# Sparse attention scores on one NeuronCore: four key blocks as two products of 64 keys or as one of 128

## The chip, the cores and the metric

The kernel runs on one core of one Trainium2 chip. The metric is the device time of one execution in microseconds (us), of which the median over several runs counts. A profile is one further execution, recorded by the hardware profiler.

## The reference

The reference is a block-sparse attention followed by a mixture of experts. There are 4 batches, 8 heads, 768 positions and 64 values per head, all in 32-bit floats. Positions form 24 blocks of 32. A query block attends to its neighbours, to the first and the last block, and to three drawn blocks; the first and the last query block attend to everything.

```python
scores = scale * np.matmul(q, k.transpose(0, 1, 3, 2))
mask = np.abs(blk_i - blk_j) <= window
mask = mask | (blk_i == 0) | (blk_j == 0) | (blk_i == n_blocks - 1) | (blk_j == n_blocks - 1)
for qb in range(n_blocks):
    for kb in sampled_blocks[qb]:
        mask[qb * block:(qb + 1) * block, kb * block:(kb + 1) * block] = True
scores = np.where(mask, scores, -1000000000.0)
...
attn = np.exp(scores)
attn = attn / (np.sum(attn, axis=-1, keepdims=True) + 1e-09)
return np.matmul(attn, v)
```

The result, as 3072 rows of 512 values, goes through a gate that picks one of 8 experts for each row. The expert is two matrix products (512 to 1024 and back) with a rectifier between them, and its result is scaled by the gate's weight.

## The kernel before

Attention comes first and the experts second; the same room in SBUF serves both. For one batch the 24 query blocks form six groups, numbered g. Groups 0 to 4 are full tiles of 128 queries: two query tiles (ti = 0 and 1) of two blocks each, with 64 queries to a tile. Group 5, called GL, holds the last two ordinary blocks and the two that attend to everything. GL is worked first in each batch.

The work of a group is cut into two half-steps of two head pairs each, so a batch has 12 half-steps and the kernel 48. The loop at L1271 runs over them. A head pair lies on the 128 partitions of keys and queries, one head on partitions 0 to 63 and the other on 64 to 127.

For each head pair of a full tile, plan (L288) lists the score products. The keys of a query tile are 384: 128 common to the group (xk: the first and the last block and the group's middle), 64 of its own neighbourhood (kT), and 192 drawn ones (kr: six blocks of 32, three for each query block). Keys are the stationary operand and queries the moving one, and the scores land in PSUM with the keys on the partitions. A product with 64 keys is put on the lower or the upper half of the PSUM partitions; plan calls the list of these few, and the list of products with 128 keys many. scores (L314) issues few for both head pairs at L321 and then many for both at L326, each product once for each head. Then ScalarE takes the exponential of the whole tile of scores (L331), and VectorE multiplies it by a mask (L337).

The drawn keys are brought to kr by place_keys (L515) two half-steps ahead: ScalarE copies the first three blocks of a query tile and VectorE the other three (both L528). The drawn values come from DRAM by indirect DMAs of the POOL queue (fetch_values, L488), each held back by a small copy (not_before, L500) until a given piece of work is done.

On TensorE the order is written out by hand and is the program's order. In a half-step it is: the scores of this half-step, the transposes of the next batch's keys or queries (turn, L156), the products of the previous half-step's probabilities with the values (attend, L355), and among these, in every second half-step, the transposes of a finished tile (turn_out, L437) and the gate's logits (L455). VectorE divides by the sums afterwards (divide, L415 to L421). In the last batch VectorE also works out where each row goes (early, L1239, and the functions it calls, among them count at L744).

After attention the experts run on tiles of 128 rows (layer1 at L1094, layer2 at L1108), with weights fetched two tiles ahead.

The functions that the change touches, and those that call them:

Of the kernel before, what the change touches and what calls it, by code (L numbers as in the profile page):

```python
# [17 lines left out]
def kernel(  # L18
# [12 lines left out]
    P = 128  # L31
    B, H, S, D = q.shape
# [246 lines left out]
    def parity(b, g):  # L279
        return (b * NG + order.index(g)) % 2  # L280
# [4 lines left out]
    def at_cols(tile_, a, n):  # L285
        return lambda r: tile_[r, a : a + n]

    def plan(b, g, pr):  # L288

        kT, qT = sets[b][0][:, pr, :], sets[b][1][:, pr, :]  # L290
        mine = [kr[:, parity(b, g), ti, pr, :] for ti in range(2)]
        q0 = BLK + P * g
        few, many = [], [(at_cols(xk[:, parity(b, g), pr, :], 0, P), at_cols(qT, q0, P), 0, P)]
        for ti in range(2):
            qs = at_cols(qT, q0 + D * ti, D)
            few += [(0, at_cols(kT, P * (g + ti), D), qs, P + D * ti, D), (1, at_cols(mine[ti], 0, D), qs, P + D * ti, D)]
            many.append((at_cols(mine[ti], D, P), qs, 2 * P + D * ti, D))
        return few, many

    def plan_all(b, pr):  # L300
# [970 lines left out]
    for i, (b, g, half) in enumerate(steps):  # L1271
# [17 lines left out]
        if g == GL:  # L1289
            plans = [plan_all(b, pr) for pr in prs if b > 0] + [plan_two(b, prs)]  # L1290
            *e_alls, e = scores(*plans)
            masked_two(e)
            mine = [(b, g, pr, e_alls[pr % 2] if b > 0 else None, e) for pr in prs]
        else:
            found = scores(*[plan(b, g, pr) for pr in prs])
            for e in found:
                masked(e, g)
            mine = [(b, g, pr, None, e) for pr, e in zip(prs, found)]
# [236 lines left out]
```

## Time and profile before

| what | us |
|---|---|
| timed runs: median of three | 679.02 |
| timed runs: lowest and highest | 676.74, 680.68 |
| profiled execution | 650.76 |
| its span, first to last instruction | 649.0 |
| attention in it, from the first scores of a half-step to the first expert product | 34.4 to 286.0 |
| TensorE matmul busy time | 611.7 |
| TensorE weight-load busy time | 512.0 |
| VectorE, ScalarE, GpSimd busy time | 300.9, 218.1, 184.1 |
| mean granted TensorE clock, as a share of full speed | 0.973 |

In the profile PE stands for TensorE's matmuls, PEld for its weight loads, which run beside matmuls, DVE for VectorE, ACT for ScalarE, POOL for GpSimd and SP for SyncE. A row of the groups gives the line, the engine, the operation, what it writes and reads, the shapes (partitions x elements), the count, the busy time with the mean duration of one in nanoseconds, and the idle time of the engine just before these instructions with what ended it. "issue" is a wait in which nothing that the profile shows was late. A row of the timeline gives the start, the time covered, the engine, the line, the operation, and how many neighbouring instructions of one kind it merges. A row of the waits gives the total, how often it came, and the longest.

### The profile page before, as it was taken

What the parts mean: (1) busy time and instruction counts of PE and PEld (TensorE: products, weight loads), DVE (VectorE), ACT (ScalarE), POOL (GpSimd) and SP (SyncE); (2) the same over time, 40 slices, a digit from 0 to 9 for tenths busy, and PEclk for the clock granted to TensorE, in tenths of its full rate; (3) what the DMA queues carried; (4) which work ended last, traced back from release to release, by engine and by line L of the source; (5) the groups of instructions that cost most, each with busy time, mean ns of one, the idle gap of its engine ahead of it and who ended that gap; (6) DMA issues with size and microseconds to landing.
All of it is one profiled execution on the core that took longest, in us unless ns stands there. A gap on an engine that the chain in (4) does not pass through costs nothing. (4 is left out here: it accounts for less than half of the span.)

```text
span 649.0 us, 21354 instructions
## 1 busy us (share of the span) xinstructions
PE 611.7 (94%) x8952; PEld 512.0 (79%) x8952; DVE 300.9 (46%) x966; ACT 218.1 (34%) x418; POOL 184.1 (28%) x289
## 2 busy tenths in 40 slices
PE   7789999998999997999999999999989999999994
PEld 6778888997999886987777777877869678867862
DVE  4247765765577488734920495202091024602200
ACT  2347755775677655431111011111111211111110
POOL 2047753552455344620111221011400212020210
PEclk9689999999999999699999999999999999999998
DMA  9889886987797338876888999869995799989950
GB/s 184 210 195 245 243 218 158 221 231 198 158 232 235 95 90 290 283 260 231 315 299 299 335 383 348 293 239 382 396 397 192 256 405 397 339 278 402 396 189 20
DMA packets 136249, 170.93 MB, mean 263 GB/s; under 512 B 83444, under 2 KB 83445, under 8 KB 136118
## 3 DMA queue, kind: packets, MB, share of 16 engines
q1 hardware_dynamic: 126080, 137.61, 65.4%
q0 software_dynamic: 10000, 31.59, 15.2%
q8 instruction: 80, 1.31, 0.9%
q14 instruction: 51, 0.42, 0.2%
q10 hardware_dynamic: 38, 0.00, 0.0%
HBM read 150.11 MB, written 19.33 MB: 261 GB/s over the span
## 5 line engine op out<-in xcount | busy, mean ns | idle before, releaser
L1094 PEld LDWEIGHTS hp<-around,room 128*128 128x128 f32 x1216 | 138.3, 192 | 7.3 <-issue 5.1
L1094 PE MATMUL hp<-around,room 128*128 128x128 f32 x1216 | 140.8, 276 | 1.4 <-ACT kr L1101 1.4
L1075 DVE STREAM_TRANSPOSE around<-xg 32x128 f32<-32x128 f32 x208 | 63.0, 303 | 125.9 <-PE hp L1094 95.9
L1108 PE MATMUL zp<-room,kr 128*128 128x512 f32 x256 | 112.7, 594 | 0.0
L488 POOL DMA_INDIRECT around<-v_rows,rows_of x88 | 92.6, 1052 | 63.5 <-DVE xk L513 25.3
L331 ACT ACTIVATE ea<-s 128x768 f32<-128x768 f32 x104 | 79.7, 809 | 91.1 <-PE s L326 70.7
L355 PE MATMUL op<-around,ea 128*64 128x65 f32 x2112 | 87.6, 228 | 5.2 <-DMA around<-v_rows,rows_of 3.9
L1108 PEld LDWEIGHTS zp<-room,kr 128*128 128x128 f32 x256 | 47.6, 191 | 54.6 <-issue 54.6
L355 PEld LDWEIGHTS op<-around,ea 128*64 128x64 f32 x2112 | 76.3, 140 | 13.3 <-DMA around<-v_rows,rows_of 4.5
L337 DVE TENSOR_TENSOR ea<-ea,mask 128x768 f32<-128x768 f32 x80 | 73.2, 954 | 14.8 <-ACT ea L331 14.8
L1101 ACT ACTIVATE kr<-hp 128x512 f32<-128x512 f32 x36 | 21.5, 597 | 117.4 <-PE hp L1094 109.9
L1123 POOL DMA_INDIRECT out_dram<-kr,sB x14 | 14.1, 1005 | 164.7 <-ACT kr L1113 106.1
L1113 ACT ACTIVATE kr<-zp,xg 128x512 f32<-128x512 f32 x16 | 11.0, 687 | 101.2 <-PE zp L1108 101.2
L1201 DVE STREAM_TRANSPOSE ea<-ea 32x128 f32<-32x128 f32 x84 | 21.7, 285 | 32.7 <-DMA ea<-x_rows,gB 32.0
L321 PE MATMUL s<-room 64*64 64x64 f32 x736 | 24.4, 237 | 5.3 <-DVE room L161 4.6
L1123 POOL DMA_INDIRECT out_dram<-kr,sA x5 | 5.1, 1020 | 79.6 <-ACT kr L1113 79.6
L326 PE MATMUL s<-other,kr 64*128 64x64 f32 x352 | 26.9, 266 | 0.7 <-issue 0.7
L321 PEld LDWEIGHTS s<-room 64*64 64x64 f32 x736 | 20.2, 147 | 7.3 <-issue 4.5
L326 PE MATMUL s<-room,kr 64*128 64x64 f32 x352 | 25.8, 261 | 0.0
L326 PEld LDWEIGHTS s<-other,kr 64*128 64x128 f32 x352 | 25.0, 195 | 0.8 <-issue 0.8
L326 PEld LDWEIGHTS s<-room,kr 64*128 64x128 f32 x352 | 23.9, 190 | 1.0 <-issue 1.0
L500 POOL COPY paced<-sums 1x1 f32<-1x1 f32 x42 | 7.5, 179 | 60.1 <-DVE sums L415 55.6
(338 smaller groups left out, 870.2 us busy)
## 6 DMA issues: line engine op xcount, KB each, us to landing
room<-in_moe_w_dram SPq DMA_DIRECT2D x46, 2048.0 KB
room<-in_moe_w_dram SPq DMA_DIRECT2D x16, 512.0 KB
room<-in_k_dram SPq DMA_DIRECT2D x32, 192.0 KB
room<-in_q_dram SPq DMA_DIRECT2D x32, 192.0 KB
x_rows<-xb SPq DMA_DIRECT2D x20, 256.0 KB
v_rows<-room SPq DMA_DIRECT2D x12, 260.0 KB
v_rows<-other SPq DMA_DIRECT2D x12, 260.0 KB
room<-in_v_dram SPq DMA_DIRECT2D x16, 192.0 KB
```

What stands on the lines that cost most here:

```text
L321: nc.tensor.matmul(s[j * D : (j + 1) * D, hh, a : a + n], lhsT=keys(r), rhs=queries(r), start=True, stop=True)
L326: nc.tensor.matmul(s[:, hh, a : a + n], lhsT=keys(r), rhs=queries(r), start=True, stop=True)
L331: nc.scalar.activation(e, s[:, :, : 6 * D], AF.Exp, scale=scale)
L337: nc.vector.tensor_tensor(e, e, m[:, None, :].to_broadcast([P, 2, 6 * D]), op=ALU.mult)
L355: nc.tensor.matmul(op[ti * D : (ti + 1) * D, pr % 2, hh, : D + 1], lhsT=e, rhs=values[:, (2 * pr + hh) * VW : (2 * pr + hh + 1) * VW], sta ...
L488: nc.gpsimd.indirect_dma_start(out=around[p0:, par, 1 + ti + 2 * ch, :], out_offset=None, in_=v_d[b][:, :], in_offset=bass.IndirectOffsetO ...
L1075: nc.vector.transpose(xT[d, :, t], xg[t, :DM].rearrange("p (c q) -> p c q", c=DB)[:, :, d])
L1094: nc.tensor.matmul(hp[:, m, :], lhsT=st[i]["w1"][:, c, fb * P : (fb + 1) * P], rhs=st[i]["xT"][:, c, :], start=(c == 0), stop=(c == DB - 1),)
L1101: nc.scalar.activation(hT[:, g * (FB // 2) : (g + 1) * (FB // 2), :], hp[:], AF.Relu)
L1108: nc.tensor.matmul(zp[:], lhsT=st[i]["hT"][:, fb, :], rhs=st[i]["w2"][:, fb, :], start=(fb == 0), stop=(fb == FB - 1),)
L1123: ins = nc.gpsimd.indirect_dma_start(out=to[:, :], out_offset=bass.IndirectOffsetOnAxis(ap=at, axis=0), in_=rows, in_offset=None, bounds_c ...
L1201: nc.vector.transpose(xT_u[d, :, j * P + tq * 32 : j * P + (tq + 1) * 32], xg_u[t, j, :DM].rearrange("p (c q) -> p c q", c=DB)[:, :, d],)
```

## The change

In plan, the 128 keys of a query tile's last four drawn blocks (columns 64 to 191 of kr) were one entry of many: one product with 128 keys and 64 queries. Now they are two entries of few with 64 keys each: columns 64 to 127 go to the lower half of the PSUM partitions and columns 128 to 191 to the upper half, at the same PSUM columns. The scores land where they landed before. They are issued at L321 with the other products of 64 keys, ahead of all products of many, of which one per head pair is left (xk). plan_two, which serves group GL, is not changed.

```diff
         for ti in range(2):
             qs = at_cols(qT, q0 + D * ti, D)
             few += [(0, at_cols(kT, P * (g + ti), D), qs, P + D * ti, D), (1, at_cols(mine[ti], 0, D), qs, P + D * ti, D)]
-            many.append((at_cols(mine[ti], D, P), qs, 2 * P + D * ti, D))
+            few += [(j, at_cols(mine[ti], D * (1 + j), D), qs, 2 * P + D * ti, D) for j in range(2)]
         return few, many
```

## The prediction

> **What bounds the kernel now.** I read the page first: shares of busy time, the groups of the changed lines, the DMA queues.
>
> ```profile
> span 649.0 us, 21354 instructions
> PE 611.7 (94%) x8952; PEld 512.0 (79%) x8952; DVE 300.9 (46%) x966; ACT 218.1 (34%) x418; POOL 184.1 (28%) x289
> ...
> q8 instruction: 80, 1.31, 0.9%
> ...
> L326 PEld LDWEIGHTS s<-room,kr 64*128 64x128 f32 x352 | 23.9, 190 | 1.0 <-issue 1.0
> ```
>
> TensorE sets the time. The chain of waits holds only the last 1.2 us and tells nothing of attention. The q8 row matters later: TensorE's own instructions arrive by DMA, 16 KB a packet. The trace shows each f32 product as two weight loads and two matmuls, so the 352 loads of a 128-key block are 176 products.
>
> Next, the timeline of TensorE's weight loads in one half-step of scores, which shows the pace of both kinds:
>
> ```profile
> 125.31 0.14 PEld L321 LDWEIGHTS s<-other,kr 64*64 64x64 f32 x2
> 125.33 0.17 PEld L321 LDWEIGHTS s<-other 64*64 64x64 f32 x2
> 125.37 0.14 PEld L321 LDWEIGHTS s<-other,kr 64*64 64x64 f32 x2
> 125.38 0.17 PEld L321 LDWEIGHTS s<-other 64*64 64x64 f32 x2
> 125.43 0.14 PEld L321 LDWEIGHTS s<-other,kr 64*64 64x64 f32 x2
> ...
> 125.55 0.14 PEld L321 LDWEIGHTS s<-other,kr 64*64 64x64 f32 x2
> 125.75 0.30 PEld L326 LDWEIGHTS s<-other,xk 64*128 64x128 f32 x4
> 125.97 0.53 PEld L326 LDWEIGHTS s<-other,kr 64*128 64x128 f32 x8
> 126.42 0.31 PEld L326 LDWEIGHTS s<-other,xk 64*128 64x128 f32 x4
> ```
>
> One load takes 0.14 us, yet four (two rows of x2) start every 0.06 us: four 64x64 quarters of the array work side by side. The single records give 58.3 ns a round of four. The eight kr loads of 128 keys take from 125.97 to 126.42, 0.446 us: 112 ns a round of two. The burst runs at the pace of its loads.
>
> Then the waits of TensorE, and one stall in its timeline:
>
> ```profile
> PE op L355 <- DMA around<-v_rows,rows_of: 3.9, 4, 1.9
> PE s L321 <- issue: 3.7, 5, 1.5
> PE xr L437 <- DVE xb L421: 3.4, 2, 2.1
> PE s L326 <- issue: 2.9, 3, 1.3
> ```
>
> ```profile
> 129.39 0.22 PE L321 MATMUL s<-other 64*64 64x64 f32 x2
> 130.34 0.27 PE L321 MATMUL s<-other,kr 64*64 64x64 f32 x2 [0.73 <-issue]
> ```
>
> Little is waited for, so denser scores should shorten the path. But what are the "issue" waits, where no semaphore is late? I counted the load and matmul records in order: eleven gaps over 0.24 us between 60 and 225 us all come where the count is 193 modulo 256, one packet of 256 instructions of 64 bytes apart. The packet records of q8 fit: the gap ending at 130.34 follows a packet that ran from 127.53 to 128.81, the one ending at 150.51 a packet to 149.19, the one at 162.54 a packet to 161.11; TensorE goes on 1.3 to 1.5 us after the packet's end. It has run out of instructions. Such gaps cost some 7.5 us now.
>
> **What the Trainium skill says.** "TensorE: Matmul & The Clock Gate", LDWEIGHTS (loading the stationary operand): the time goes with the columns, P / 1.2 ns, 53 for 64 and 107 for 128. The trace agrees, 58 and 112 a round. "TensorEngine Tiling (Array Packing)", Tiling Modes: a 64x64 mode has four tiles that load and multiply in parallel, and a change of mode drains the array. The trace agrees: rounds of four, and 0.20 us from the last 64-key load (125.55) to the first 128-key one (125.75). "Runtime: NRT & Kernel Launch", Instruction fetch mechanics: instructions come in 16 KiB blocks of 256, the next fetched while the current one runs, and this is hidden. The block size agrees; "hidden" does not, by the eleven gaps.
>
> **The change, part by part.** It touches plan, so 40 of the 48 half-steps (4 batches, 5 full tiles, 2 halves); the others use plan_two.
>
> Removed: per half-step two plans x two tiles of queries x two heads x two loads = 16 loads of 128 keys: 2 x 0.446 = 0.89 us. Added: 32 loads of 64 keys in the first loop, 8 rounds x 58.3 ns = 0.47 us. Bounds for the added rounds: 58 ns as existing 64-key rounds run, or 112 if they lost the side-by-side order; I take 58, since the new list alternates halves and heads as the old one does. Saved 0.425 x 40 = 17.0 us. The mode changes stay as many.
>
> Moved: the products of key blocks 2 to 5 now precede the 128-key middles. They read kr, of which VectorE copies half (L528); in this half-step those copies for a later burst end at 126.94 and that burst starts at 129.16, so 2.2 us of cover and no cost. No DMA, POOL or SP instruction moves. ScalarE's first exponential waits for its plan's last product: 0.47 us of extra 64-key rounds come before it and 0.45 us of kr loads go, so it starts as before; the second comes 0.43 earlier. The masked result is ready at 129.36 and read at 132.7, with a stall of 0.9 between: no cost; without that cover 0.4 us a step.
>
> Block fetch: two half-steps hold 504 load and matmul records in 9.2 us (115.6 to 124.8), so 256 last 4.7 us. After, 568 in 8.4 us, so 256 last 3.8 us, and attention has five blocks more (1,280 records). From the q8 records, measured from TensorE's entry into a block, the next packet starts 0.2 to 3.4 us later (median 1.5), runs 1.1, and is usable 1.4 after: 4.1 us in all on average, 3.3 to 5.3 for eight in ten of 49. This is below a block's time now and above it afterwards. The mean excess of these 49 times over 4.7 us is 0.13, over 3.8 us it is 0.5. With 29 ordinary blocks in the first three batches this was 29 x 0.13 = 3.8 us, and becomes 33 x 0.5 = 16.5; the slower last batch goes from 10 x 0.05 to 11 x 0.2, 0.5 to 2.2. That is 14.4 more; the same arithmetic gives 11 us for the stalls of before, of which the trace has 7.5, so it may be a third too high. Lower bound 5 (times 0.4 us shorter), upper 22 (0.2 to 0.3 us longer). I take 13.
>
> Last batch: between 227 and 262 us TensorE waits for VectorE, which routes tokens there (xb 3.4 us, ea and cnA some 1.5). The saving of the six half-steps ahead of those waits, 6 x 0.43 = 2.6 us, turns into a longer wait (0 to 4).
>
> Gathers (L488): they land 5.4 us after issue (median), and the fourth of each tile has under 1 us to spare in about one tile of three. Part of a half-step's saving comes off that margin; 0.5 us (0 to 2).
>
> Sum: -17.0 + 13 + 2.6 + 0.5 = -0.9. The profiled execution is 650.8 us, its span 649.0. It would be 649.9. The timed runs have a median 28 us above it, for a reason that no view shows; I carry the difference over in us: 679.0 - 0.9, say 678.0. The expected gain goes into waits for instructions.
>
> **Rivals.** (1) *The blocks stay hidden.* If the 1.5 us before a packet starts is mostly queueing behind data that happens to be there, and shrinks by 0.5 us or more, only the VectorE and gather terms are left: -17.0 + 2.6 + 0.5, up to 13.9 us faster, 665; half of it, 671. For it: 38 of 49 blocks come in time now. Against it: the DMA row of the page reads 7 to 9 through attention. (2) *The instruction fetch becomes the bound and costs more than the saving.* After a late block the next request leaves only when TensorE resumes; in the eleven such cases the packet started 1.7 us later on average, not 1.5. With 0.25 us more a block the excess over 3.8 us rises from 0.5 to 0.68, and 44 blocks give 8 us more: 7 us slower, 686. It passes the half-per-cent mark from about 0.15 us. For it: at the three second half-steps of a last tile, with long runs of 64-key products (blocks of 2.7 us), the wait came each time, 0.7 to 1.3 us. Against it: before has fewer stalls than its own spread of times suggests. (3) *The change doesn't do what it says:* four quarters don't overlap for the new products, rounds stay at 112 ns; nothing saved, more blocks, some 8 us slower. Unlikely, since kr loads at L321 already run at 58.
>
> **How the numbers follow.** Likeliest, the fetch takes back nearly all: 0.42, own range 675 to 682. Rival 1: 0.26. Rivals 2 and 3: 0.32. A measurement of this kernel can tell about 0.5% (3.4 us) from no change. Of the likeliest case 0.02 falls on either side: faster 0.28, same 0.38, slower 0.34. Range 668.5 to 686.
>
> **What would show it.** From first to last matmul start the scores of a half-step take 1.49 us, not 1.91, where no gap falls into them; L321 has 1,280 loads more, and L326's kr rows keep 64 loads in all, those of plan_two. "Issue" waits of TensorE rise from 7 to some 20 us, in more than 20 gaps 256 records apart. Waits for xb rise. If the issue waits stay near 7, rival 1 holds; if they pass 25, rival 2. Wrong would be the pace of the 64-key rounds, or a wait on kr in front of L321.

## The result, and the profile after

| what | before | after |
|---|---|---|
| timed runs, median of four each, side by side (us) | 679.06 | 695.26 |
| lowest and highest | 676.74, 680.68 | 694.29, 696.72 |
| profiled execution, its span | 650.76, 649.0 | 694.29, 692.6 |
| attention in it, to the first expert product | 286.0 | 327.1 |
| mean granted TensorE clock | 0.973 | 0.95 |

The ratio is 1.0252 [1.0213, 1.0292]: 16.2 us slower, where the prediction had 0.9 us faster and a range that ended 7 us above the kernel before. The profiled spans lie further apart than that, by 43.6 us, and 41.1 of these are attention: from the first expert product on the span has 365.5 us after and 363.0 before.

From the page of the changed kernel: span and busy time, the clock in 40 slices, the instruction queue, and one group of the new products.

```profile
span 692.6 us, 22635 instructions
PE 633.9 (92%) x9592; PEld 521.7 (75%) x9592; DVE 300.6 (43%) x966; ACT 216.0 (31%) x418; POOL 182.6 (26%) x289
...
PEclk9799999988998999958999999999999999999998
...
q8 instruction: 85, 1.39, 0.8%
...
L321 PE MATMUL s<-room,kr 64*64 64x64 f32 x992 | 34.6, 232 | 9.4 <-issue 9.2
```

The counts are those of the prediction: 640 matmuls and as many loads more, and five packets of instructions more (85, not 80); this group has 992 matmuls, 640 more than before, and a second one like it reads other,kr. What is new stands in the last column: 9.2 us of "issue" in this group alone. TensorE's waits:

```profile
PE s L321 <- issue: 21.2, 50, 0.9
...
PE op L355 <- issue: 4.5, 13, 0.5
```

"Issue" at L321 was 3.7 us in 5 waits of up to 1.5; it is 21.2 in 50, none over 0.9. More of the old stall would be longer or more of the same length; these are many and short. The timeline of TensorE's matmuls in one such burst:

```profile
124.08 0.23 PE L321 MATMUL s<-other,kr 64*64 64x64 f32 x2
124.12 0.23 PE L321 MATMUL s<-other 64*64 64x64 f32 x2
124.14 0.23 PE L321 MATMUL s<-other,kr 64*64 64x64 f32 x2
124.62 0.21 PE L321 MATMUL s<-other,kr 64*64 64x64 f32 x1 [0.26 <-issue]
125.35 0.21 PE L321 MATMUL s<-other,kr 64*64 64x64 f32 x1 [0.52 <-issue]
126.09 0.29 PE L321 MATMUL s<-other,kr 64*64 64x64 f32 x2 [0.53 <-issue]
126.82 0.29 PE L321 MATMUL s<-other,kr 64*64 64x64 f32 x2 [0.44 <-issue]
```

After half a burst at full pace TensorE stands still four times, some 0.73 us apart, with only 2 to 4 records of loads and matmuls between. These are not the stalls that the prediction counted: they do not come 256 records apart. Counted from one start to the next, the load and matmul records of this profile have 68 such pauses, 39.7 us in all. The stalls that the prediction counted, in which a block of instructions came late, are fewer here than in the kernel before: 7 with 3.8 us.

The later runs below come from other occasions, on three chips, on which the kernel before takes 652 to 656 us and not 679. There the pauses never came, in either kernel. So two things have to be told apart: what the change costs on those occasions, and what it cost on the first one.

### The profile page after: what moved, and what is told of

It reads as the page before. It is cut to its first block, busy times and chain, and to the rows that moved or that the text cites. A ratio compares the mean times of both kernels' runs of the same rounds, so it can differ in the third digit from the quotient of the medians.

```text
span 692.6 us, 22635 instructions
## 1 busy us (share of the span) xinstructions
PE 633.9 (92%) x9592; PEld 521.7 (75%) x9592; DVE 300.6 (43%) x966; ACT 216.0 (31%) x418; POOL 182.6 (26%) x289
## 3 DMA queue, kind: packets, MB, share of 16 engines
q0 software_dynamic: 10000, 31.59, 14.5%
## 5 line engine op out<-in xcount | busy, mean ns | idle before, releaser
L488 POOL DMA_INDIRECT around<-v_rows,rows_of x88 | 90.7, 1031 | 59.8 <-DVE xk L513 24.9
L355 PE MATMUL op<-around,ea 128*64 128x65 f32 x2112 | 97.9, 243 | 4.8 <-issue 3.8
L355 PEld LDWEIGHTS op<-around,ea 128*64 128x64 f32 x2112 | 85.3, 154 | 15.7 <-issue 10.3
L1123 POOL DMA_INDIRECT out_dram<-kr,sB x14 | 14.1, 1005 | 167.2 <-ACT kr L1113 106.1
L321 PE MATMUL s<-room,kr 64*64 64x64 f32 x992 | 34.6, 232 | 9.4 <-issue 9.2
L321 PE MATMUL s<-room 64*64 64x64 f32 x736 | 34.6, 240 | 7.2 <-DVE room L161 4.6
L321 PE MATMUL s<-other,kr 64*64 64x64 f32 x992 | 33.4, 236 | 5.9 <-issue 5.9
L321 PE MATMUL s<-other 64*64 64x64 f32 x736 | 34.2, 230 | 4.4 <-issue 3.8
L321 PEld LDWEIGHTS s<-room,kr 64*64 64x64 f32 x992 | 27.8, 143 | 12.6 <-issue 12.3
L321 PEld LDWEIGHTS s<-room 64*64 64x64 f32 x736 | 26.7, 149 | 9.9 <-issue 7.4
L321 PEld LDWEIGHTS s<-other,kr 64*64 64x64 f32 x992 | 27.7, 148 | 7.6 <-issue 7.4
L500 POOL COPY paced<-sums 1x1 f32<-1x1 f32 x42 | 9.0, 213 | 92.1 <-DVE sums L415 87.4
```

The source lines that it names most:

```text
L321: nc.tensor.matmul(s[j * D : (j + 1) * D, hh, a : a + n], lhsT=keys(r), rhs=queries(r), start=True, stop=True)
L355: nc.tensor.matmul(op[ti * D : (ti + 1) * D, pr % 2, hh, : D + 1], lhsT=e, rhs=values[:, (2 * pr + hh) * VW : (2 * pr + hh + 1) * VW], sta ...
L488: nc.gpsimd.indirect_dma_start(out=around[p0:, par, 1 + ti + 2 * ch, :], out_offset=None, in_=v_d[b][:, :], in_offset=bass.IndirectOffsetO ...
L1123: ins = nc.gpsimd.indirect_dma_start(out=to[:, :], out_offset=bass.IndirectOffsetOnAxis(ap=at, axis=0), in_=rows, in_offset=None, bounds_c ...
```

## The experiments

Three theories. **A**: TensorE's instructions are supplied at a limited mean rate, about one load or matmul in 17 ns, and the new products ask for more. **B**: a run of 128 such records at 7 ns each is too long for what lies ready in front of TensorE, so that the pauses belong to the changed kernel. **C**, the prediction's own mechanism, that blocks of 256 instructions come late, with one thing that the prediction did not have: after a longer wait TensorE runs at a lower clock.

Ratios are to the kernel before on the same chip. A late block is a gap of over 0.24 us between the starts of two loads or matmuls, at a count of 193 modulo 256. The count takes in TensorE's own semaphore and branch instructions; without them the place drifts, in the kernel before from 169 to 145 (the prediction says "load and matmul records", which is not enough). "Attention to" gives the time of the first expert product. The expectations of e1 to e4 start from 679 us, but on these occasions the kernel before takes some 654, so only their differences and ratios can be held against the results.

**e1_before_again.** The kernel before, unchanged.

> The kernel before, unchanged. Its profiled execution took 651 us and its timed runs 679, and the profiled one has none of the pauses of 0.6 to 0.7 us, one after the other inside the 64-key rounds, that the changed kernel shows. Theory A (TensorE's instructions arrive at a limited mean rate, near 59 records per us, and the changed kernel asks for 67) and theory B (a run of 128 records at 7 ns each is too long, whatever the mean): about 679 us, and if the 28 us between timed and profiled execution are such pauses, this trace shows them too, fewer than after. If they are something else, the trace has none and a span near 649.

Measured: 652.69 us, 0.9989 [0.9956, 1.0023]; attention to 291.0; 12 late blocks, 11.8 us. So the stall of before is a property of the kernel, not of one execution.

**e5_after_again.** The changed kernel, unchanged.

> The changed kernel, unchanged. In its first profile some 35 us went into pauses of 0.6 to 0.7 us that no run of the second set of times shows, nor either profile of the kernel before. If those pauses belong to the changed kernel (theory B): 690 to 697 against 654 for before, ratio 1.06, and the trace shows them. If they belong to the occasion and the change itself costs by late blocks of instructions and by lower clock after such waits (theory C): ratio 1.01 to 1.03, 661 to 674, no such pauses, and some 20 gaps 256 records apart that cost about 20 us.

Measured: 661.65 us, 1.0110 [1.0028, 1.0191]; attention to 294.2; 20 late blocks, 22.1 us; no pauses of the first kind. TensorE's waits, first e1, then e5:

```profile
PE s L321 <- issue: 6.3, 8, 2.0
PE op L355 <- DMA around<-v_rows,rows_of: 4.0, 3, 1.7
PE s L326 <- issue: 2.7, 3, 1.0
```

```profile
PE s L321 <- issue: 10.1, 10, 1.7
PE op L355 <- issue: 7.5, 7, 2.0
PE op L355 <- DMA around<-v_rows,rows_of: 6.8, 6, 3.0
```

Here the waits for instructions grow as the prediction had it: from 9.2 us (with 0.2 at L355) to 17.6, few and long. B falls as it was put: the same program runs without the pauses. One late block of e5 in the timeline:

```profile
121.61 0.32 PE L321 MATMUL s<-other,kr 64*64 64x64 f32 x4
123.51 0.34 PE L321 MATMUL s<-other,kr 64*64 64x64 f32 x6 [1.57 <-issue]
```

The packet of instructions ran from 120.97 to 122.11; TensorE goes on at 123.51, 1.40 us after its end, as in the kernel before.

**e2_half.** Only the first query tile of each group is split.

```diff
-            many.append((at_cols(mine[ti], D, P), qs, 2 * P + D * ti, D))
+            if ti == 0:
+                few += [(j, at_cols(mine[ti], D * (1 + j), D), qs, 2 * P + D * ti, D) for j in range(2)]
+            else:
+                many.append((at_cols(mine[ti], D, P), qs, 2 * P + D * ti, D))
```

> Only the first query tile of each full tile gets the split (32 added records a half-step in place of 64; runs of 96 in place of 128). Theory A: 61 records per us asked for, just over the limit: between no change and half of the change's loss, 679 to 687. Theory B: runs of 96 exceed what is queued less often, 683 to 690. Theory C (late blocks of 256 instructions alone, as predicted): 676 to 680.

Measured: 660.03 us, 1.0111 [1.0062, 1.0159], no less than for the whole change; 20 late blocks, 24.4 us. The profiled execution (665.9 us of span, 40 us of attention at half clock, against 14 to 27 in the kernel before and in e5) is slower than the timed ones, so I read only its count of late blocks. The loss is as large as that of the whole change. C forecast at most 1 us of loss and missed; the measured 5.5 us between the medians lie within the 0 to 8 that A forecast.

**e3_both.** The new products are added and the old ones kept; the same scores are computed twice. Against the changed kernel:

```diff
             few += [(j, at_cols(mine[ti], D * (1 + j), D), qs, 2 * P + D * ti, D) for j in range(2)]
+            many.append((at_cols(mine[ti], D, P), qs, 2 * P + D * ti, D))
```

> The 64-key products are added and the 128-key products are kept (the same scores are computed twice). The records of a burst's first part are those of the changed kernel, a run of 128, but the mean demand is only 57 per us, since 0.47 us of work is added to each half-step. Work alone: 679 + 19 = 698. Theory A: no pauses beyond those of before, 696 to 702. Theory B: the pauses of the changed kernel come as well, 16 + 17 us more for what they take now: 720 to 735.

Measured: 680.25 us, 1.0449 [1.0386, 1.0511]; attention to 310.8, 22.8 us more than the mean of three profiles of the kernel before. TensorE's records without gaps give 19.9 us more of scores (40 half-steps x 8 rounds x 58.3 ns = 18.7 were to be expected), late blocks 18 with 18.9 us, some 8 us more.

```profile
PE s L322 <- issue: 7.4, 8, 2.3
PE op L356 <- DMA around<-v_rows,rows_of: 3.7, 2, 2.9
PE s L327 <- issue: 4.0, 5, 1.0
```

The pace of the added rounds is right, and to them comes what late blocks cost. Two half-steps now hold 632 load and matmul records in some 10.1 us, 62 per us and not the 57 of the expectation (504 in 9.2 us before, 568 in 8.4 after the change), so instructions are still asked for faster than before; the run does not tell A from C. What it shows is that 64-key rounds that replace nothing cost more than their array time: 22.8 us of attention for 18.7.

**e4_late.** The new products go behind the products of 128 keys, in a third loop of scores.

```diff
+            late += [(j, at_cols(mine[ti], D * (1 + j), D), qs, 2 * P + D * ti, D) for j in range(2)]
...
+        for s, (_, _, late) in zip(ss, plans):
+            for j, keys, queries, a, n in late:
...
```

> The changed kernel's products in another order: the old 64-key ones, the 128-key ones, then the new 64-key ones. Runs of 64 records as before, mean demand 64 per us (8 us of further mode changes). Theory A: pauses as in the changed kernel, a little fewer: 693 to 702. Theory B: no pauses: -17 + 8 + some 6 for later blocks, 674 to 679.

Measured: 666.54 us, 1.0216 [1.0166, 1.0265]; attention to 301.4; 22 late blocks, 23.4 us. Two bursts of 64-key products in place of one do not help. The scores without gaps are only some 5.7 us below those of before, where the changed kernel's are 12.6 below. The third loop brings one more change between 128-key and 64-key products in a half-step, and the undisturbed scores of a half-step take 1.75 us, not 1.53 as in the changed kernel. The late blocks stay.

**e6_before_noload and e7_after_noload.** The kernel before and the changed one with fewer transfers in attention: queries and keys of batches 1 to 3 are not loaded (what lies in the staging room is transposed in their place), and batches 2 and 3 use the values of batches 0 and 1. TensorE's program in attention stays the same.

```diff
-            out=around[p0:, par, 1 + ti + 2 * ch, :], out_offset=None, in_=v_d[b][:, :],
+            out=around[p0:, par, 1 + ti + 2 * ch, :], out_offset=None, in_=v_d[b % 2][:, :],
...
-                if here < 6:
-                    fill_next(b + 1, here + 2)
-        if b + 2 < B and here >= 8:
-            fill_next(b + 2, here - 8)
...
-        if b + 1 < B:
+        if b == 0:
```

> The kernel before without the loads of queries and keys for batches 1 to 3 and without the loads and the stores of values for batches 2 and 3 (old contents are used in their place; other rows go to the experts). The transposes stay. Theory C: instruction blocks come sooner, gaps 256 records apart fall from 10 gaps and 8 us to under 3 us; attention ends 5 to 12 us earlier. Theory B: no effect of loads on gaps.

> The changed kernel with the same loads and stores left out. Theory C: the blocks come in time here as well, and the change now shows its 17 us less waits for VectorE: attention ends 8 to 16 us earlier than in the kernel before without these loads, timed ratio 0.975 to 0.99 to it. Theory B, or a limit on the rate of instructions that has nothing to do with the loads: attention ends later than in that kernel, as it does with the loads.

Measured: e6 678.94 us, 1.0359 [1.0264, 1.0454], with 2 late blocks of 1.5 us, attention to 280.9; e7 676.58 us, 1.0329 [1.0233, 1.0426], with 13 late blocks of 13.0 us, attention to 276.3. Other rows go to other experts in these two, so the experts take longer (some 400 us, not 363) and they are to be compared with each other alone. **The sign has turned**: e7 is 4.6 us faster in attention and 2.4 in the timed medians. That is less than the 8 to 16 us that C expected of e7, and its blocks do not all come in time as C had it. Two views: TensorE's waits in e6 and in e7.

```profile
PE s L326 <- issue: 1.0, 2, 0.6
```

```profile
PE s L321 <- issue: 6.6, 7, 1.7
...
PE op L355 <- issue: 1.7, 3, 0.8
PE s L326 <- issue: 1.5, 1, 1.5
```

With less data beside them, the packets of instructions start earlier: from TensorE's entry into a block to the packet's start the median is 0.70 us in e6 and 1.09 in e7 (1.1 in e10 and e11 below), against 1.53 in the kernel before and 1.59 in e5.

**e8_late_batches.** Split only in batches 2 and 3, where fewer transfers run.

```diff
-            many.append((at_cols(mine[ti], D, P), qs, 2 * P + D * ti, D))
+            if b >= 2:
+                few += [(j, at_cols(mine[ti], D * (1 + j), D), qs, 2 * P + D * ti, D) for j in range(2)]
+            else:
+                many.append((at_cols(mine[ti], D, P), qs, 2 * P + D * ti, D))
```

> The change in batches 2 and 3 alone, where fewer loads run beside attention. Theory C: batch 2 gains 1 to 3 us of its 4.3, batch 3 loses most to VectorE: 651 to 656, ratio 0.995 to 1.003. Theory B, or a cost the same in every batch: half the change's loss, ratio 1.01 to 1.015.

Measured: 658.97 us, 1.0101 [1.0067, 1.0134]; 16 late blocks, 19.8 us, in a profile (653.6 us of span) that lies below its timed median. My guess from C missed: half the change, in what I took for the lighter batches, costs as much as the whole, as far as the intervals tell. The trace shows where: in the first two batches, which are as before, late blocks take 6.0 us (6.6 in the mean of three profiles of the kernel before), and in the two that are split 13.8 (4.1 before). Half the saving, 6.6 us, meets 9.7 us of further stalls. So late blocks come where the products are split. Taken with e2, the loss does not grow with the number of products that are split, at least not evenly.

**e9_after_third, e10_before_bare, e11_after_bare.** The changed kernel, e6 and e7 once more, on another chip and with more rounds, since the turn of the sign is small.

> The changed kernel as it is, once more. Theory C (late blocks of 256 instructions, as the prediction has it) expects about 20 late blocks with 20 us of gaps in one profile and a ratio to the kernel before of 1.008 to 1.02. Theory B (the pauses of 0.7 us inside the scores belong to the changed kernel) expects at least 30 of them here, and a ratio near 1.025.

> The kernel before without the loads of q and k from the second batch on and of v and the stores from the third on. Beside e11 alone it decides: theory C expects hardly any late blocks (0 to 4) here.

> The changed kernel with the same transfers left out. Theory C expects the sign to turn: 2 to 8 us below e10, since late blocks still cost up to 13 us of the 17 saved. Theory A (a limited mean rate of supply, whatever else moves) expects it 4 to 10 us above e10, as with the transfers.

Measured: e9 662.69 us, 1.0148 [1.0084, 1.0212], 23 late blocks, 28.3 us, no pauses. e10 680.24 us, 1.0416 [1.0356, 1.0475], 4 late blocks, 3.3 us, attention to 279.3; e11 675.44 us, 1.0367 [1.0308, 1.0427], 9 late blocks, 8.1 us, attention to 273.1. TensorE's waits in e10, then in e11:

```profile
PE s L326 <- issue: 1.4, 2, 0.7
...
PE s L321 <- issue: 0.8, 1, 0.8
```

```profile
PE s L321 <- issue: 5.1, 6, 1.7
...
PE s L326 <- issue: 1.1, 1, 1.1
```

Again the changed kernel is faster without the transfers, by 6.2 us in attention and 4.8 timed; from the six single runs of each I work out 0.995 [0.989, 1.000]. By itself this could still be no change; with the transfers the same edit costs 1.1 to 1.5% on the same two chips. A expected e11 4 to 10 us above e10, and it is below. The batches agree. In the two middle ones the DMA engines are busy for 0.75 and 0.73 of the time in e5 and for 0.40 and 0.41 in e7, and late blocks take some 14 us in each of e5, e9 and e13 but 3.0 in e7 and 2.0 in e11. In the last batch the share stays (0.67 and 0.66), and so do the late blocks: 1.7, 6.9 and 4.9 us with the transfers, 6.5 and 4.2 without.

**e12_before_elsewhere, e13_after_elsewhere.** Both kernels unchanged, in search of an occasion with pauses.

> The kernel before, unchanged. If the pauses of 0.7 us belong to the occasion and not to the change, then wherever this kernel takes near 679 us its profile shows them too, some 25 us in total; where it takes 648 to 661 us it shows none, with 8 to 15 late blocks at most.

> The changed kernel, unchanged, beside e12. Where e12 takes 648 to 661 us: no pauses, about 20 late blocks, 658 to 668 us. Where e12 takes near 679: pauses in both and some 695 us. If the pauses belong to the changed kernel, they are here and not in e12.

Measured: 654.29 and 661.33 us in one execution each, 9 late blocks (10.9 us) and 20 (27.4 us), no pauses of the first kind. A third chip gives a difference of 7 us, from one execution of each (9 us against a second execution of the kernel before, 652.07). TensorE's waits in e13:

```profile
PE s L321 <- issue: 14.3, 11, 2.1
PE op L355 <- issue: 7.6, 6, 2.0
```

## Why the prediction was wrong

There are three profiles of each kernel without pauses. In each I added up, from 34.0 us to the first expert product, the intervals from one load or matmul start to the next: gaps of over 0.24 us before an instruction that waits for no semaphore, those before one that does, and the rest by what TensorE does. Nearly all gaps of the first kind are late blocks; a late block can fall before an instruction of the second kind too, so late blocks alone sum to 10.8 us in the mean before and 25.9 after.

| us | before, e1, e12 | mean | e5, e9, e13 | mean | difference |
|---|---|---|---|---|---|
| scores, without gaps | 104.8, 104.4, 102.3 | 103.8 | 91.4, 91.7, 90.5 | 91.2 | -12.6 |
| gaps, no semaphore to wait for | 9.5, 10.9, 9.7 | 10.0 | 20.2, 28.3, 26.8 | 25.1 | +15.1 |
| gaps, a semaphore to wait for | 12.3, 14.1, 14.5 | 13.6 | 19.7, 13.3, 15.3 | 16.1 | +2.5 |
| products with the values | 90.6, 92.1, 91.9 | 91.5 | 92.5, 93.7, 91.2 | 92.5 | +1.0 |
| transposes and logits | 34.8, 35.5, 34.9 | 35.1 | 36.5, 36.3, 36.1 | 36.3 | +1.2 |
| sum | 252.0, 257.0, 253.1 | 254.0 | 260.2, 263.4, 260.0 | 261.2 | +7.2 |

The spans differ by 8.4 us (651.9 and 660.3); the 1.2 outside attention is the wait for the experts' first weights, 2.4 us before and 3.7 after. The timed medians differ by 7.8, 6.6 and 7 us on three chips. So **on these occasions the change costs some 7 us**, where the prediction's sum was -0.9. Step by step:

- *The pace of 64-key rounds: right.* Where no gap and no lower clock falls into them, the scores of a half-step take 1.53 us, not 1.91 (predicted 1.49).
- *"Saved 0.425 x 40 = 17.0 us": too much, and one of the terms that failed.* It is 0.38 x 40 = 15.2 by the undisturbed bursts, and 12.6 in all. The rest goes in bursts in which a block came late, 1.61 us without their gaps, and in those at a lower clock, 1.6 to 2.4 us.
- *Late blocks, "I take 13": right in mechanism, +15.1.* The count doubles, from 9 to 12 to 20 to 23, and the gaps lie where they were expected. It is within the bounds of 5 and 22. (The stalls of before, 7.5 us in the prediction, are 10.0 by this count. The 11 us that the prediction gives for them as a check do not follow from the terms it shows, 3.8 and 0.5.) The two pairs e6, e7 and e10, e11 support the reason given: take transfers out, and the gaps fall from 10.0 to 2.6 us (kernel before) and from 25.1 to 10.4 (changed kernel), while the scores still save 14.7. The sum turns to -5.4. Which transfers delay the packets was not tried.
- *VectorE in the last batch, 2.6: not there.* The waits for xb are 3.4, 2.4 and 1.3 us before and 2.0, 1.6 and 3.3 after.
- *Gathers, 0.5: small, as said.* Waits for v_rows are 4.1 us in the mean before and 5.0 after.
- *Left out: +2.2 in work that the change does not touch.* The prediction counted a stall as its gap alone. But TensorE runs at half clock for stretches of 3.4 us, one or several, nearly all of which begin around a wait of 1.3 us or more: in e13 at 72.4, 150.9 and 212.4 us, just after late blocks of 2.3, 1.9 and 2.2 us. Some half of the waits of that length have no such stretch beside them. Stretches that follow a late block are none, two and one in the profiles of before, and one, three and three in e5, e9 and e13. In all, attention has 20.1 us at half clock in the mean before and 25.0 after; half of the 4.9 between them is an estimate of what they cost, 2.4 us. The three profiles of before differ among themselves by more (13.7, 23.9 and 22.8), so that the clock is the cause of the +2.2 is likely, not shown. "TensorE: Matmul & The Clock Gate", Part 1: The HAM clock gate, says that the clock is granted by how busy TensorE was recently, at half rate or full. The traces agree: every stretch in them is granted at 0.5 or 1.0, in multiples of 3.4 us.
- *Smaller slips.* The DMA row of the page, read as 7 to 9 through attention, has 6 to 9 and two slices at 3; half of rival 1's gain gives 672, not 671. Neither enters the sum.

So the step that failed, against the 7 us, is the sum of saving and stalls: the saving of 17.0 was too large by 4.4, the stalls of 13 too small by 2, and 2.2 of slower work was not in it; waits for semaphores took 2.5 of the 3.1 allowed. In amount this is rival 2 (7 us slower), but not by its mechanism: from TensorE's entry into a block until it is usable (the end of its packet and 1.4 us) it takes 4.26 us in the mean of the three profiles before and 4.23 after. The blocks did not come later; they were wanted earlier. Against "Runtime: NRT & Kernel Launch", Instruction fetch mechanics, for which the fetch is mostly hidden, 20 to 23 of the 53 or 54 blocks of attention are not.

**The first occasion.** There the change cost 16.2 us, twice as much. The kernel before took 679 us, 23 to 27 more than elsewhere, and the changed one 695, 33 to 34 more. The profile of the kernel before, 650.8 us, was not one of those runs and has no pauses, so what held the timed runs of before back by these us is seen in no profile, and the step "I carry the difference over in us" failed: it took 28 us of unknown cause for a constant that the change leaves alone. Of the 17 us between prediction and measurement 8 are the sum above, and 9 stand against this step. The same sums for the first profile of the changed kernel give: scores 98.5, gaps with no semaphore to wait for 44.1, with one 15.7, products with the values 97.4, the rest 37.5, in all 293.1 us, with 51 us at half clock. Against e5, e9 and e13 it is 32 us longer. The pauses stand at any place within a block of 256, so they are no late blocks. That pauses and the time of 679 us go together fits all runs, but no run met them again; what causes the pauses, and whether the kernel before has them too, **stays open**.

**Theories.** C holds for the 7 us: shown by the count and place of the gaps, by the batches of e8, and by the two pairs without the transfers (e6 and e7, e10 and e11); its share of lower clock is not shown. A falls as their cause, since the same demand for instructions leaves far fewer gaps when transfers are taken out. B falls as it was put, since the same program runs without the pauses; that they need both the changed kernel and that occasion is not excluded. In e8 late blocks account for the loss of half the change, but why they grow by 9 and 14 us with half of the products split (e8 and e2), against 15 with all, is not settled, and C's sums did not foresee it. No version with all transfers is faster than the kernel before.

## What to carry to other kernels

Before splitting products to run side by side on TensorE, count instructions, not only array time: here 256 of them were used up in less time than the 4.2 us in which the next 256 came, and each late block took a microsecond or two. Look for "issue" waits that recur every 256 instructions, TensorE's semaphore instructions counted in; if there are some already, a denser burst is paid back in such waits. And where timed runs and the profile of a kernel differ by 28 us, find that out first: what makes them differ can also change what an edit is worth.

## What the runs showed of the hardware

- A packet of 16 KB of instructions takes 0.9 to 1.5 us in most cases; where TensorE waits for it, it goes on some 1.4 us after its end. The delay from TensorE's entry into a block to the packet's start was 1.3 to 1.6 us (median of a profile), and 0.7 to 1.1 when other transfers were taken out.
- A further change between 64-key and 128-key products in a half-step cost 0.21 us (e4, scores without gaps).
- Stretches at half clock began within 2 us after single late blocks of 1.8 to 2.3 us, ten times in six profiles; other late blocks as long had none.
- Pauses of 0.3 to 0.7 us, about 0.73 us apart, inside a burst of products, mostly with 2 to 10 records between them: 68 in one profile, no series of them in the thirteen later ones.
